# Attention and ELU feed-forward on one core: row sums issued together with the first half of AV, q and k copied from PSUM in one pass, loads and steps of the start reordered, dummy matmuls moved

## The chip, the core and the metric

The kernel runs on one core of a Trainium2 chip. The metric is the device time of one launch in microseconds (us); lower is better. A core has a tensor engine (PE, matrix products into the PSUM memory), a vector engine (DVE), a scalar engine (ACT), GpSimd (POOL, here it only makes masks and issues loads) and SyncE (SP, it issues the output stores). All five run at the same time, each its own list of instructions in order; semaphores join them. Times from the profile count from the start of the execution's span, which is some 1.7 us shorter than the time that is measured from outside.

## The reference

Attention over 8 batches of 8 heads, 576 queries, 16 "beacon" keys in front of 576 causal ones, head size 64; then a feed-forward layer with ELU on the 4608 x 512 result.

```python
k_all = concatenate([beacon_k, k]); v_all = concatenate([beacon_v, v])
scores = where(causal, -1e9, q @ k_all.T / 8)          # B,H = 8,8; S = 576; D = 64
a = exp(scores - max); a /= a.sum(-1) + 1e-9
x = (a @ v_all) laid out as [4608, 512]
h = x @ w_in                                           # 512 -> 2048
g = where(h > 0, h, exp(min(h, 0)) - 1)
out = g @ w_out                                        # 2048 -> 512
```

## The kernel before

The program is a list of small *steps*. Each step puts instructions on one engine, and the order of the list is the order of every engine's own program. `b` is a batch, `p` a pair of heads, `g` a part, `t` a tile of 512 tokens, `i` a piece of it.

- `T.b.p` (PE) transposes q and k of a pair into PSUM; `ck` (ACT) copies k out of PSUM, `cq` (DVE) copies q; `cb` (DVE) puts the beacon keys in front.
- `S.b.p.g` (PE) scores, `x` (ACT) exp, `m` (DVE) causal mask.
- `L.b.g` (PE) row sums of the exps, by a product with ones; `n` (ACT) turns them into 1/sum as exp(-Ln(sum)), so it holds the Ln; `W.b.g.half` (PE) product with v for one half of the head size (AV); `M` (DVE) multiplies AV by 1/sum into x. `R` (PE) does sums and AV for the last 64 queries, which do not fit one bank.
- `F.t.i` (PE) x @ w_in; `e` (ACT) exp; `r`, `g` (DVE) ELU; `G.t.tb.qd` (PE) g @ w_out; `o` (DVE), `s` (SP) copy and store.
- `lk`, `lv`: loads of q and k, of v. `warm.n`: n matmuls with zeros that only keep PE running.

The parts that the change and the argument touch (cuts marked `...`):

```python
psum = tc.tile_pool(name="psum", bufs=2, space=PSUM)   # tags: "S" 2 pairs of banks, "hps" 2 banks, "ops" 2 banks
...
new_stage(0); load_qk(0, ...) x4; new_stage(1); load_v(0, ...)
load_qk(1, 0, H // 2); load_wi(0, 1024); load_wi(1024, 2048); load_qk(1, H // 2, H)
load_wo(0); load_wo(1); load_wo(2); load_wo(3)
load_v(1, list(range(NKC)))
...
def T(b, p):
    if b == 0 and p < 3:
        tps[b, p] = bank("hps", BF16, "tq"), bank("hps", BF16, "tk")
    else:
        t = psum.tile([P, 2, 1024], BF16, tag="S", name="tp")    # one pair of banks: q and k
        tps[b, p] = t[:, 0, :], t[:, 1, :]
    ...
def ck(b, p):
    nc.scalar.copy(out=kTof[b, p][:, NB:SK]..., in_=tps[b, p][1][:, 0:S]...)
def cq(b, p):
    nc.vector.tensor_copy(out=qTof[b, p]..., in_=tps[b, p][0][:, 0:S]...)
def S_(b, p, g):
    ...
    if b == 0:
        nc.tensor.matmul(out=s[:, 0, :], lhsT=zero[:, 0:P], rhs=zero, ...)   # a dummy
    ...
def L(b, g):
    ...
    t = psum.tile([P, 2, 512], FP32, tag="S", name="lt")
    quad(b, g, 0, Q1, t[:, 0, :], None, True)
    lt[b, g], ut[b, g, 0] = t[:, 0, :], t[:, 1, :]     # sums in one bank, AV half 0 in the other
def W(b, g, *i):
    ...
    if half:
        t = psum.tile([P, 2, 512], FP32, tag="S", name="ut")
        ut[b, g, 1], ut[b, "R"] = t[:, 0, :], t[:, 1, :]   # AV half 1 in one bank, R in the other
    quad(b, g, 0, Q1, ut[b, g, half], half, True)
...
run(""" warm.12 bt bk cb.0.0 cb.0.1 T.0.0 ... (the start: some 420 steps by hand, batches 0 to 2) ... """)

def LW(b, g):
    run(f"L.{b}.{g} n.{b}.{g} W.{b}.{g}.0 M.{b}.{g}.0")
def WR(b, g):
    run(f"W.{b}.{g}.1 M.{b}.{g}.1")
    if g == 1:
        run(f"R.{b} n.{b}.R M.{b}.R")

SLOTS = [0, 1, 2, 4, 5, 6, 8, 9, 10, 11, 12, 13]
for b in range(3, NT // TT + 2):                       # the loop: one turn for one tile of tokens
    for i in range(NFC):                               # 16: F.b.i e r g, G of tile b-1, and at the slots:
        # SC(b,1,0) SC(b,1,2) T_(b,3)+LW(b,0) SC(b,2,0) SC(b,2,2) T_(b+1,0)+WR(b,0)
        # SC(b,3,0) SC(b,3,2) T_(b+1,1)+LW(b,1) SC(b+1,0,0) SC(b+1,0,2) T_(b+1,2)+WR(b,1)
```

Both PSUM pairs of `L` and `W` are one tile for the program. A step of one engine on a tile waits for the earlier steps of other engines on it, although they are at the other bank.

The softmax here doesn't subtract the row's maximum and nothing guards it: scores larger than these inputs give would overflow.

## Time and profile before

403.2 us, median of 3 runs (402.68 to 404.11).

| | before |
|---|---|
| span of the profiled run | 400.2 us |
| PE, DVE, ACT busy | 91%, 68%, 57% |
| the loop begins (first F of turn 3) | 113.1 us |
| a turn of the loop (turns 3 to 6) | 43.49 us |
| first F at all | 30.4 us |

PE does nearly all the time's work, so the question is where PE does not work. The page of the profile: busy us and instructions of each engine; then PE in 40 slices of the span (tenths; 9 is 90% or more) and the clock of PE that was granted.

```profile
PE 365.4 (91%) x4416; PEld 183.8 (46%) x4416; DVE 270.8 (68%) x640; ACT 227.6 (57%) x351; POOL 67.8 (17%) x100
...
PE   6889859989899998999899989999899999999995
...
PEclk9899969999999999999999999999999999999999
```

There is a hole near the sixth slice (50 to 60 us), with the clock low, and single 8s among the 9s of the loop. The waits of PE before: who waited for whom, us in total, times, longest.

```profile
PE lt L304 <- ACT rl L337: 8.9, 12, 0.9
PE ut L304 <- DVE xT L374: 7.0, 5, 1.5
PE tp L229 <- DMA qst<-in_q_dram: 3.1, 1, 3.1
PE tp L229 <- DMA kst<-in_k_dram: 2.1, 1, 2.1
PE sc L259 <- DVE qT L250: 1.9, 2, 1.1
...
PE sc L267 <- ACT kT_94 L243: 1.4, 2, 1.0
```

The first line is W.0 waiting for Ln, the second is R waiting for M, and both recur in the loop. The next two are T.2.0 waiting for q and k of batch 2; the last two are scores that wait for the copies `cq` and `ck`. The timeline of PE in turn 3 of before (start us, us of the group, ..., idle time ahead of it and its releaser) shows the two waits of the loop:

```profile
120.11 0.76 PE L304 MATMUL lt<-et,ones 128*32 128x512 f16 x20
121.59 0.76 PE L304 MATMUL lt<-et,v_1838 128*32 128x512 f16 x20 [0.72 <-ACT rl L337]
...
149.76 0.76 PE L304 MATMUL ut<-et,v_1838 128*32 128x512 f16 x20
152.01 0.48 PE L304 MATMUL ut<-et,ones 128*32 128x64 f16 x40 [1.50 <-DVE xT L374]
```

And stretches of before: us, then busy us of PE, PE weight loads, DVE, ACT, POOL (instructions), granted clock, DMA share (time of the packets over that of the 16 engines; it can pass 1), GB/s. The stretches are: first F to T.2.0, the wait at T.2.0, from there to the loop, and one turn.

```profile
30.40:49.10 18.70, 17.84 (x254) 12.07 (x252) 14.75 (x42) 15.69 (x24) 9.48 (x13) 1.00 1.50 191
49.10:55.60 6.50, 1.37 (x25) 1.06 (x26) 0.96 (x2) 0.86 (x1) 3.07 (x4) 0.70 1.32 204
55.60:113.10 57.50, 54.01 (x895) 30.13 (x894) 43.87 (x109) 39.88 (x63) 7.68 (x11) 0.97 0.61 75
156.60:200.10 43.50, 40.56 (x530) 19.95 (x529) 31.38 (x75) 27.23 (x42) 6.27 (x10) 1.00 0.49 67
```

### The profile page before, as it was taken

To read this page: it belongs to the slowest core of one execution; us is meant where nothing else is said; L and a number is where in the kernel's file an instruction comes from. 1 tells how busy PE (TensorE), PEld (TensorE's weight loads), DVE (VectorE), ACT (ScalarE), POOL (GpSimd) and SP (SyncE) were. 2 spreads that over 40 slices of the span, in tenths; PEclk is the share of its full clock that TensorE was granted. 3 is DMA by queue.
4 is the path that set the end of the run, shared out by engine and by line. 5 is a ranking of instruction groups with operands and counts; after the bars stand their busy time and mean duration, and the time that the engine had idled before them with its cause. 6 is when DMAs were issued, how large, how long until landed. Compare 5 with 4: busy or idle time off the path is not lost.

```text
span 400.2 us, 10284 instructions
## 1 busy us (share of the span) xinstructions
PE 365.4 (91%) x4416; PEld 183.8 (46%) x4416; DVE 270.8 (68%) x640; ACT 227.6 (57%) x351; POOL 67.8 (17%) x100
## 2 busy tenths in 40 slices
PE   6889859989899998999899989999899999999995
PEld 3347535544454444444444444444444444444442
DVE  2447826778786876776677776777677667767741
ACT  2889736678566664667466656667366533333300
POOL 8784520410041004100330004000000000000000
PEclk9899969999999999999999999999999999999999
DMA  8999997491098007830297009000001000010112
GB/s 121 172 187 198 184 200 51 56 148 60 29 62 146 28 29 53 118 87 7 40 88 134 28 29 89 28 26 28 25 5 54 20 34 27 29 52 26 55 52 79
DMA packets 61102, 28.84 MB, mean 72 GB/s; under 512 B 41088, under 2 KB 55424, under 8 KB 61056
## 3 DMA queue, kind: packets, MB, share of 16 engines
q0 software_dynamic: 54720, 18.49, 41.6%
q1 hardware_dynamic: 5760, 9.57, 6.5%
q8 instruction: 34, 0.56, 0.6%
q10 hardware_dynamic: 576, 0.13, 0.2%
q14 instruction: 12, 0.10, 0.1%
HBM read 37.22 MB, written 9.44 MB: 117 GB/s over the span
## 4 chain that ended last, share of the span: by engine, by line
PE 76%; DMA 8%; POOL 5%; ACT 4%; DVE 4%; issue 2%; POOLq 0%
PE hps L425 30%; PE ops L456 29%; PE sc L267 6%; PE lt L304 5%; DMA kst<-in_k_dram 4%; DMA w_out_80<-in_moe_w_out_dram 4%; PE ut L304 3%; PE tp L229 3%; ACT rl L337 2%; ACT et L277 1%; DVE qT L250 1%; POOL w_in_79 L138 1%; POOL v_124 L126 1%; DVE xT L374 1%; POOL qst L113 1%
## 5 line engine op out<-in xcount | busy, mean ns | idle before, releaser
L425 PE MATMUL hps<-xT,w_in_79 128*128 128x512 f16 (+1 forms) x640 | 148.8, 361 | 0.3
L456 PE MATMUL ops<-w_out_80,gt 128*128 128x512 f16 x576 | 145.1, 379 | 0.0
L435 ACT ACTIVATE e<-hps 128x512 f32<-128x512 f32 x144 | 86.3, 600 | 86.4 <-PE hps L425 86.0
L277 ACT ACTIVATE et<-sc 128x832 f16<-128x832 f32 x128 | 104.4, 863 | 19.4 <-PE sc L267 19.1
L447 DVE TENSOR_TENSOR gt<-hps,r 128x512 f16<-128x512 f32 x144 | 99.6, 691 | 6.2 <-PE sc L267 0.5
L456 PEld LDWEIGHTS <-gt 128*128 128x128 f16 x576 | 55.9, 98 | 66.5 <-issue 0.5
L440 DVE TENSOR_SCALAR r<-e 128x512 f16<-128x512 f32 x144 | 61.4, 427 | 36.7 <-ACT e L435 35.4
L425 PEld LDWEIGHTS <-w_in_79 128*128 128x128 f16 x640 | 56.8, 98 | 56.3 <-issue 5.1
L293 DVE TENSOR_TENSOR et<-et,triu 128x256 f16<-128x256 f16 (+3 forms) x164 | 40.7, 270 | 30.2 <-ACT et L277 30.1
L250 DVE COPY qT<-tp 128x576 bf16<-128x576 bf16 x29 | 21.9, 757 | 15.1 <-ACT kT_94 L243 8.3
L463 DVE COPY osb<-ops 128x512 f32<-128x512 f32 x36 | 24.5, 682 | 10.2 <-PE ops L456 10.2
L374 DVE TENSOR_TENSOR xT<-lt,rl 128x448 f16<-128x448 f32 (+6 forms) x28 | 10.6, 418 | 9.9 <-PE lt L304 9.5
L304 PEld LDWEIGHTS <-ones 128*32 128x32 f16 (+1 forms) x624 | 10.8, 96 | 12.0 <-issue 8.7
L229 PE MATMUL tp<-identb,qst 96*64 96x96 bf16 x348 | 13.1, 212 | 3.2 <-DMA qst<-in_q_dram 3.1
L229 PEld LDWEIGHTS <-qst 96*64 96x64 bf16 x384 | 10.3, 111 | 12.5 <-issue 8.6
L229 PE MATMUL tp<-identb,kst 96*64 96x96 bf16 x348 | 12.5, 209 | 2.1 <-DMA kst<-in_k_dram 2.1
L340 ACT ACTIVATE rl<-rl 128x512 f32<-128x512 f32 (+2 forms) x23 | 12.4, 537 | 0.7
L113 POOL DMA_DIRECT2D qst<-in_q_dram x12 | 8.7, 726 | 21.0 <-PE tp L229 16.6
L304 PE MATMUL lt<-et,ones 128*32 128x512 f16 (+7 forms) x320 | 11.8, 279 | 0.2 <-DVE qT L250 0.2
L229 PEld LDWEIGHTS <-kst 96*64 96x64 bf16 x384 | 10.7, 112 | 2.5 <-DMA kst<-in_k_dram 2.3
L337 ACT ACTIVATE rl<-lt 128x512 f32<-128x512 f32 (+1 forms) x15 | 9.0, 603 | 3.4 <-PE lt L304 2.5
L374 DVE TENSOR_TENSOR xT<-ut,rl 128x448 f16<-128x448 f32 (+6 forms) x28 | 10.4, 414 | 0.6 <-ACT rl L337 0.6
(95 smaller groups left out, 231.1 us busy)
## 6 DMA issues: line engine op xcount, KB each, us to landing
out_dram<-osb SPq DMA_DIRECT2D x36, 256.0 KB, 2.0
qst<-in_q_dram POOLq DMA_DIRECT2D x6, 576.0 KB, 6.2
kst<-in_k_dram POOLq DMA_DIRECT2D x6, 576.0 KB, 8.5
w_in_79<-in_moe_w_in_dram POOLq DMA_DIRECT2D x16, 128.0 KB, 5.1
w_out_80<-in_moe_w_out_dram POOLq DMA_DIRECT2D x4, 512.0 KB, 12.3
qst<-in_q_dram POOLq DMA_DIRECT2D x4, 144.0 KB, 4.5
kst<-in_k_dram POOLq DMA_DIRECT2D x4, 144.0 KB, 5.0
qst<-in_q_dram POOLq DMA_DIRECT2D x2, 288.0 KB, 6.0
```

The costliest lines, as they stand in the source:

```text
L229: nc.tensor.transpose(out=dst[D * h:D * (h + 1), PR * r:PR * (r + 1)], in_=src[:, 2 * p + h, r, :], identity=identb[0:PR, 0:PR],)
L250: nc.vector.tensor_copy(out=qTof[b, p].rearrange("c (p r) -> c p r", r=R), in_=tps[b, p][0][:, 0:S].rearrange("c (r p) -> c p r", r=R))
L277: nc.scalar.activation(out=ets[b, p][:, :, GW * g:GW * (g + 1)], in_=sc[b, p, g][:, :, 0:GW], func=AFT.Exp, bias=0.0, scale=SCALE)
L293: nc.vector.tensor_tensor(out=o, in0=o, in1=triu[0:kc[j], :, t0:t0 + e - a], op=ALU.mult)
L304: nc.tensor.matmul(out=t[32 * i:32 * (i + 1), a - qa:e - qa], lhsT=ones[0:kc[j], :] if half is None else v16[0:kc[j], j, h, 32 * half:32 * ...
L374: nc.vector.tensor_tensor(out=x_tile(k)[:, cc, tok - TT * k:to - TT * k], in0=u[:, o:o + to - tok], in1=r[:, o:o + to - tok], op=ALU.mult)
L425: nc.tensor.matmul(out=h[:, n_, :], lhsT=w_in16[:, cc, P * fc:P * (fc + 1)], rhs=xt[k][:, cc, a - TT * k:e - TT * k], start=(cc == 0), sto ...
L435: nc.scalar.activation(out=eb[t, i], in_=flat(hp[t, i]), func=AFT.Exp, bias=0.0, scale=1.0)
L440: nc.vector.tensor_scalar(out=rb[t, i], in0=eb[t, i], scalar1=1.0, scalar2=1.0, op0=ALU.min, op1=ALU.subtract)
L447: nc.vector.tensor_tensor(out=flat(gt), in0=flat(hp[t, i]), in1=rb[t, i], op=ALU.max)
L456: nc.tensor.matmul(out=ob[t, tb_], lhsT=gts[t, fc][:, P * tb_:P * (tb_ + 1)], rhs=w_out16[:, fc, :], start=(fc == 0), stop=(fc == NFC - 1))
L463: nc.vector.tensor_copy(out=osb, in_=ob[t, tb_])
```

## The change

Its intent: take the two waits out of the loop by order alone (W.0 before Ln; R before M), take one of two copies per pair away, bring q and k of batch 2 sooner, and spend PE's idle moments of the start on dummies that were placed for it, not in front of every score.

```diff
-    kTs = [konst.tile([P, P * NKC], BF16, name=f"kT{i}") for i in range(NKT)]
+    qks = [konst.tile([P, 2, P * NKC], BF16, name=f"qk{i}") for i in range(NQK)]
...
     load_qk(1, H // 2, H)
-    load_wo(0)
-    load_wo(1)
-    load_wo(2)
-    load_wo(3)
-    load_v(1, list(range(NKC)))
...
+    w0 = bank("ops", name="w0")
     @step
-    def warm(n):
-        w = bank("ops", name="w0")
+    def warm(n, rows=P):
         for _ in range(n):
-            nc.tensor.matmul(out=w, lhsT=zero[:, 0:P], rhs=zero, ...)
+            nc.tensor.matmul(out=w0, lhsT=zero[0:rows, 0:P], rhs=zero[0:rows, :], ...)
...
     def ck(b, p):
-        nc.scalar.copy(out=kTof[b, p][:, NB:SK]..., in_=tps[b, p][1][:, 0:S]...)
+        t = qkT[b, p]
+        if b == 0 and p < 3:
+            nc.scalar.copy(out=t[:, 1, NB:SK]..., in_=tps[b, p][1][:, 0:S]...)
+        else:                                              # q and k at once
+            nc.scalar.copy(out=t[:, :, NB:SK]..., in_=tps[b, p][:, :, 0:S]...)
...
     def S_(b, p, g):
-        if b == 0:
-            nc.tensor.matmul(out=s[:, 0, :], lhsT=zero[:, 0:P], rhs=zero, ...)
...
     run("""
-    warm.12 bt bk cb.0.0 cb.0.1 T.0.0 cb.0.3 cb.0.2 ck.0.0 cq.0.0 S.0.0.0 T.0.1 cq.0.1 x.0.0.0
+    warm.12 bt bk cb.0.0 cb.0.1 cb.0.3 cb.0.2 warm.3 T.0.0 ck.0.0 cq.0.0 warm.4.64 S.0.0.0 S.0.0.1
...
+    warm.2.64 T.0.3 wo.0 wo.1 lv.1 lk.2 wo.2 wo.3 m.0.0.3 x.0.1.2 S.0.1.3 ck.0.2 m.0.1.0 m.0.1.2
... (the rest of the start in a new order; 24 dummies of 64 rows in it; q's copies gone but three)
     def LW(b, g):
-        run(f"L.{b}.{g} n.{b}.{g} W.{b}.{g}.0 M.{b}.{g}.0")
+        run(f"L.{b}.{g} W.{b}.{g}.0 n.{b}.{g} M.{b}.{g}.0")
     def WR(b, g):
-        run(f"W.{b}.{g}.1 M.{b}.{g}.1")
-        if g == 1:
-            run(f"R.{b} n.{b}.R M.{b}.R")
+        run(f"W.{b}.{g}.1" + g * f" R.{b}" + f" M.{b}.{g}.1" + g * f" n.{b}.R M.{b}.R")
-    SLOTS = [0, 1, 2, 4, 5, 6, 8, 9, 10, 11, 12, 13]
+    SLOTS = [0, 1, 2, 4, 5, 6, 7, 8, 9, 11, 12, 13]
```

The texts below speak of 26 small dummies; the list of after has 24.

More of the change, by code (lines that the diff above doesn't have):

```diff
@@ L152 @@
     nc.vector.memset(ones, 1.0)
-    NKT = 4
-    kTs = [konst.tile([P, P * NKC], BF16, name=f"kT{i}") for i in range(NKT)]
-    for kt in kTs:
-        nc.vector.memset(kt[:, SK:P * NKC], 0.0)
+    NQK = 4
+    qks = [konst.tile([P, 2, P * NKC], BF16, name=f"qk{i}") for i in range(NQK)]
+    for t in qks:
+        nc.vector.memset(t[:, 1, SK:P * NKC], 0.0)
     identb = konst.tile([P, P], BF16)
@@ L194, in bank @@
         return psum.tile([P, 512 if dt == FP32 else 1024], dt, tag=tag, name=name)
+    w0 = bank("ops", name="w0")
     @step
-    def warm(n):
-        w = bank("ops", name="w0")
+    def warm(n, rows=P):
         for _ in range(n):
-            nc.tensor.matmul(out=w, lhsT=zero[:, 0:P], rhs=zero, start=True, stop=True, skip_group_check=True)
+            nc.tensor.matmul(
+                out=w0, lhsT=zero[0:rows, 0:P], rhs=zero[0:rows, :], start=True, stop=True, skip_group_check=True)
     tb = []
@@ L214, in bk @@
         nc.vector.tensor_copy(out=bkT, in_=tb[0][:, 0:NP * P])
-    tps, kTof, qTof, sc, ets = {}, {}, {}, {}, {}
-    kseq = [0]
+    tps, qkT, sc, ets = {}, {}, {}, {}
+    seq = [0]
     @step
@@ L222, in T @@
             tps[b, p] = bank("hps", BF16, "tq"), bank("hps", BF16, "tk")
+            dsts = tps[b, p]
         else:
-            t = psum.tile([P, 2, 1024], BF16, tag="S", name="tp")
-            tps[b, p] = t[:, 0, :], t[:, 1, :]
-        for dst, src in zip(tps[b, p], st[b]):
+            tps[b, p] = psum.tile([P, 2, 1024], BF16, tag="S", name="tp")
+            dsts = tps[b, p][:, 0, :], tps[b, p][:, 1, :]
+        for dst, src in zip(dsts, st[b]):
             for r in range(R):
@@ L236, in cb @@
     def cb(b, p):
-        kTof[b, p] = kTs[kseq[0] % NKT]
-        kseq[0] += 1
-        nc.vector.tensor_copy(out=kTof[b, p][:, 0:NB], in_=bkT[:, p, NB * b:NB * (b + 1)])
+        qkT[b, p] = qks[seq[0] % NQK]
+        seq[0] += 1
+        nc.vector.tensor_copy(out=qkT[b, p][:, 1, 0:NB], in_=bkT[:, p, NB * b:NB * (b + 1)])
     @step
     def ck(b, p):
-        nc.scalar.copy(
-            out=kTof[b, p][:, NB:SK].rearrange("c (p r) -> c p r", r=R),
-            in_=tps[b, p][1][:, 0:S].rearrange("c (r p) -> c p r", r=R))
+        t = qkT[b, p]
+        if b == 0 and p < 3:
+            nc.scalar.copy(
+                out=t[:, 1, NB:SK].rearrange("c (p r) -> c p r", r=R),
+                in_=tps[b, p][1][:, 0:S].rearrange("c (r p) -> c p r", r=R))
+        else:
+            nc.scalar.copy(
+                out=t[:, :, NB:SK].rearrange("c i (p r) -> c i p r", r=R),
+                in_=tps[b, p][:, :, 0:S].rearrange("c i (r p) -> c i p r", r=R))
     @step
     def cq(b, p):
-        qTof[b, p] = attn.tile([P, S], BF16, tag="qT", bufs=4, name="qT")
         nc.vector.tensor_copy(
-            out=qTof[b, p].rearrange("c (p r) -> c p r", r=R),
+            out=qkT[b, p][:, 0, NB:SK].rearrange("c (p r) -> c p r", r=R),
             in_=tps[b, p][0][:, 0:S].rearrange("c (r p) -> c p r", r=R))
@@ L257, in S_ @@
         s = sc[b, p, g] = psum.tile([P, 2, 512], FP32, tag="S", name="sc")
-        if b == 0:
-            nc.tensor.matmul(out=s[:, 0, :], lhsT=zero[:, 0:P], rhs=zero, start=True, stop=True, skip_group_check=True)
-        qT, kT = qTof[b, p], kTof[b, p]
+        t = qkT[b, p]
         c0, c1 = GW * g, GW * (g + 1)
@@ L268, in S_ @@
                     out=s[:, h, a - c0:e - c0],
-                    lhsT=kT[D * h:D * (h + 1), P * j:P * (j + 1)],
-                    rhs=qT[D * h:D * (h + 1), qa + a - col:qa + e - col],
+                    lhsT=t[D * h:D * (h + 1), 1, P * j:P * (j + 1)],
+                    rhs=t[D * h:D * (h + 1), 0, NB + qa + a - col:NB + qa + e - col],
                     start=True, stop=True, skip_group_check=True,
@@ L471, in lk, with wo @@
     @step
+    def wo(i):
+        load_wo(i)
+    @step
     def lk(b):
@@ L487 @@
     run("""
-    warm.12 bt bk cb.0.0 cb.0.1 T.0.0 cb.0.3 cb.0.2 ck.0.0 cq.0.0 S.0.0.0 T.0.1 cq.0.1 x.0.0.0
-    S.0.0.1 ck.0.1 x.0.0.1 m.0.0.0 S.0.0.2 x.0.0.2 S.0.1.0 S.0.1.1 x.0.1.0 T.0.2 x.0.1.1 T.0.3
-    ck.0.2 S.0.0.3 m.0.0.2 ck.0.3 x.0.0.3 m.0.1.0 cq.0.3 S.0.1.2 S.0.1.3 cb.1.0 x.0.1.2 x.0.1.3
-    S.0.3.0 cq.0.2 x.0.3.0 m.0.0.3 S.0.2.0 x.0.2.0 m.0.1.2 cb.1.1 m.0.1.3 S.0.3.1 m.0.3.0 S.0.3.2
-    x.0.3.1 S.0.3.3 x.0.3.2 m.0.2.0 x.0.3.3 S.0.2.1 x.0.2.1 L.0.A W.0.A.0 cb.1.2 m.0.3.2 T.1.0 n.0.A
@@ L493 @@
-    ck.1.0 S.0.2.2 m.0.3.3 cq.1.0 W.0.A.1 S.0.2.3 x.0.2.2 x.0.2.3 S.1.0.0 M.0.A.0 M.0.A.1 m.0.2.2
-    cb.1.3 W.0.B.0.0 T.1.1 m.0.2.3 x.1.0.0 cq.1.1 W.0.B.0.1 ck.1.1 S.1.0.1 S.1.1.0 x.1.0.1 x.1.1.0
-    F.0.0 m.1.0.0 e.0.0 m.1.0.1 m.1.1.0 F.0.1 r.0.0 S.1.0.2 e.0.1 L.0.B x.1.0.2 g.0.0 n.0.B F.0.2
-    r.0.1 g.0.1 F.0.3 m.1.0.2 M.0.B.0.0 e.0.2 S.1.1.1 S.1.0.3 M.0.B.0.1 e.0.3 cb.2.0 W.0.B.1.0
-    x.1.1.1 r.0.2 g.0.2 r.0.3 W.0.B.1.1 g.0.3 S.1.1.2 M.0.B.1.1 x.1.0.3 F.0.5 F.0.4 x.1.1.2 e.0.5
-    M.0.B.1.0 T.1.2 lk.2 m.1.1.2 r.0.5 e.0.4 g.0.5 T.1.3 F.0.6 m.1.1.1 cq.1.2 ck.1.2 r.0.4 S.1.1.3
@@ L499 @@
-    ck.1.3 G.0.0.0 cq.1.3 x.1.1.3 S.1.3.0 cb.2.1 g.0.4 e.0.6 m.1.0.3 S.1.3.1 x.1.3.0 r.0.6 F.0.7
-    G.0.1.0 x.1.3.1 e.0.7 S.1.2.0 S.1.2.1 x.1.2.0 g.0.6 x.1.2.1 F.1.2 m.1.3.0 m.1.1.3 m.1.3.1 e.1.2
-    r.0.7 g.0.7 m.1.2.0 G.0.0.1 m.1.2.1 r.1.2 S.1.2.2 T.2.0 x.1.2.2 F.1.0 g.1.2 S.1.3.2 ck.2.0 e.1.0
-    cq.2.0 S.1.2.3 x.1.3.2 m.1.2.2 x.1.2.3 cb.2.2 r.1.0 g.1.0 F.1.4 G.0.0.2 e.1.4 m.1.3.2 m.1.2.3
-    r.1.4 S.2.0.0 g.1.4 T.2.1 F.1.1 x.2.0.0 ck.2.1 m.2.0.0 cq.2.1 G.0.1.1 S.2.0.1 L.1.0 e.1.1 r.1.1
@@ L504 @@
-    x.2.0.1 g.1.1 n.1.0 m.2.0.1 W.1.0.0 T.2.2 F.1.5 ck.2.2 F.1.7 cq.2.2 M.1.0.0 e.1.5 r.1.5 S.1.3.3
-    x.1.3.3 g.1.5 S.2.0.2 G.0.0.3 cb.2.3 S.2.0.3 m.1.3.3 e.1.7 F.1.3 x.2.0.2 x.2.0.3 W.1.0.1 o.0.0
-    lk.3 L.1.1 cb.3.0 W.1.1.0 r.1.7 m.2.0.2 g.1.7 M.1.0.1 e.1.3 n.1.1 W.1.1.1 lv.2 m.2.0.3 R.1 r.1.3
-    n.1.R g.1.3 M.1.1.0 F.1.6 G.0.1.2 e.1.6 M.1.1.1 S.2.2.0 M.1.R r.1.6 x.2.2.0 S.2.1.0 g.1.6
-    m.2.2.0 F.2.2 F.2.0 x.2.1.0 e.2.2 m.2.1.0 S.2.1.1 S.2.1.2 e.2.0 r.2.2 x.2.1.1 g.2.2 r.2.0 g.2.0
-    m.2.1.1 x.2.1.2 G.1.0.0 G.1.0.1 T.2.3 T.3.0 ck.2.3 F.2.1 m.2.1.2 cq.2.3 S.2.3.0 cq.3.0 ck.3.0
@@ L510 @@
-    e.2.1 S.2.2.1 G.0.1.3 r.2.1 F.2.4 x.2.3.0 g.2.1 x.2.2.1 e.2.4 S.2.1.3 m.2.3.0 o.0.1 S.2.3.1
-    m.2.2.1 cb.3.2 F.2.3 r.2.4 x.2.3.1 G.1.0.2 e.2.3 x.2.1.3 g.2.4 F.2.7 m.2.3.1 r.2.3 g.2.3 S.2.2.2
-    m.2.1.3 e.2.7 S.2.3.2 r.2.7 s.0.0 F.2.5 g.2.7 x.2.3.2 m.2.3.2 x.2.2.2 G.1.1.0 F.2.6 m.2.2.2
-    e.2.5 r.2.5 S.3.0.0 S.2.3.3 G.1.0.3 e.2.6 x.3.0.0 g.2.5 r.2.6 g.2.6 x.2.3.3 lv.3 F.2.9 S.3.0.1
-    e.2.9 x.3.0.1 m.3.0.0 o.1.0 m.2.3.3 S.2.2.3 x.2.2.3 cb.3.1 F.2.11 r.2.9 g.2.9 G.1.1.1 S.3.0.2
-    e.2.11 s.1.0 S.3.0.3 m.3.0.1 F.2.8 m.2.2.3 G.1.1.2 x.3.0.2 r.2.11 g.2.11 m.3.0.2 x.3.0.3 F.2.13
@@ L516 @@
-    m.3.0.3 G.1.1.3 e.2.8 e.2.13 r.2.8 g.2.8 F.2.10 r.2.13 g.2.13 T.3.1 e.2.10 ck.3.1 s.0.1 L.2.1
-    W.2.1.0 n.2.1 o.1.1 cq.3.1 r.2.10 L.2.0 n.2.0 g.2.10 W.2.0.0 F.2.12 M.2.1.0 e.2.12 F.2.14 e.2.14
-    W.2.0.1 M.2.0.0 s.1.1 W.2.1.1 r.2.12 R.2 g.2.12 M.2.0.1 T.3.2 r.2.14 g.2.14 ck.3.2 M.2.1.1 n.2.R
-    F.2.15 cq.3.2 e.2.15 M.2.R r.2.15 g.2.15
+    warm.12 bt bk cb.0.0 cb.0.1 cb.0.3 cb.0.2 warm.3 T.0.0 ck.0.0 cq.0.0 warm.4.64 S.0.0.0 S.0.0.1
+    T.0.1 x.0.0.0 cq.0.1 m.0.0.0 x.0.0.1 S.0.0.2 warm.1.64 S.0.0.3 ck.0.1 x.0.0.2 cb.1.0 warm.1.64
@@ new lines @@
+    T.0.2 S.0.1.0 x.0.0.3 x.0.1.0 warm.1.64 S.0.1.1 m.0.0.2 cq.0.2 x.0.1.1 warm.2.64 S.0.1.2
+    warm.2.64 T.0.3 wo.0 wo.1 lv.1 lk.2 wo.2 wo.3 m.0.0.3 x.0.1.2 S.0.1.3 ck.0.2 m.0.1.0 m.0.1.2
+    ck.0.3 warm.5.64 S.0.3.0 x.0.1.3 warm.2.64 S.0.2.0 cb.1.1 x.0.3.0 m.0.1.3 x.0.2.0 m.0.3.0
+    warm.2.64 S.0.3.1 warm.2.64 S.0.2.1 x.0.3.1 m.0.2.0 x.0.2.1 warm.2.64 S.0.3.2 x.0.3.2 L.0.A
+    S.0.3.3 n.0.A x.0.3.3 cb.1.3 m.0.3.2 W.0.A.1 T.1.0 M.0.A.1 m.0.3.3 W.0.A.0 S.0.2.2 W.0.B.0.1
+    ck.1.0 M.0.A.0 x.0.2.2 S.0.2.3 cb.1.2 T.1.1 x.0.2.3 m.0.2.2 S.1.0.0 ck.1.1 m.0.2.3 F.0.0 e.0.0
@@ new lines @@
+    r.0.0 F.0.3 x.1.0.0 g.0.0 m.1.0.0 W.0.B.1.1 e.0.3 S.1.0.1 S.1.1.0 x.1.0.1 F.0.2 r.0.3 x.1.1.0
+    e.0.2 g.0.3 L.0.B m.1.0.1 m.1.1.0 n.0.B S.1.1.1 F.0.1 r.0.2 g.0.2 F.0.5 M.0.B.0.1 M.0.B.1.1
+    x.1.1.1 S.1.1.2 S.1.0.2 W.0.B.0.0 m.1.1.1 e.0.1 r.0.1 x.1.1.2 e.0.5 W.0.B.1.0 lv.2 g.0.1 x.1.0.2
+    M.0.B.0.0 S.1.0.3 F.0.7 x.1.0.3 e.0.7 cb.2.0 T.1.2 r.0.5 m.1.1.2 m.1.0.2 ck.1.2 T.1.3 g.0.5
+    m.1.0.3 r.0.7 F.0.4 ck.1.3 g.0.7 e.0.4 M.0.B.1.0 S.1.1.3 F.0.6 cb.2.1 x.1.1.3 G.0.0.0 lk.3 r.0.4
+    g.0.4 e.0.6 m.1.1.3 r.0.6 S.1.3.0 S.1.3.1 x.1.3.1 g.0.6 F.1.1 m.1.3.1 e.1.1 x.1.3.0 G.0.1.0
@@ new lines @@
+    F.1.0 r.1.1 g.1.1 S.1.3.2 e.1.0 m.1.3.0 r.1.0 x.1.3.2 S.1.2.0 x.1.2.0 F.1.2 G.0.0.1 g.1.0 e.1.2
+    S.1.3.3 S.1.2.1 m.1.3.2 F.1.5 m.1.2.0 x.1.3.3 cb.2.2 x.1.2.1 r.1.2 S.1.2.2 e.1.5 g.1.2 F.1.3
+    m.1.3.3 G.0.1.1 x.1.2.2 m.1.2.1 r.1.5 e.1.3 g.1.5 m.1.2.2 S.1.2.3 r.1.3 T.2.0 x.1.2.3 ck.2.0
+    g.1.3 F.1.6 F.1.7 S.2.0.0 S.2.0.1 e.1.6 cb.3.0 x.2.0.0 x.2.0.1 G.0.0.2 S.2.0.2 m.1.2.3 x.2.0.2
+    G.0.1.2 T.2.1 r.1.6 g.1.6 e.1.7 m.2.0.0 T.2.2 m.2.0.1 ck.2.1 m.2.0.2 G.0.0.3 ck.2.2 L.1.0 r.1.7
+    W.1.0.0 g.1.7 S.2.0.3 o.0.0 n.1.0 cb.2.3 F.1.4 M.1.0.0 x.2.0.3 e.1.4 m.2.0.3 G.0.1.3 r.1.4
@@ new lines @@
+    W.1.0.1 o.0.1 L.1.1 M.1.0.1 g.1.4 W.1.1.0 n.1.1 W.1.1.1 M.1.1.0 R.1 S.2.1.0 M.1.1.1 x.2.1.0
+    G.1.1.0 n.1.R m.2.1.0 M.1.R F.2.1 F.2.0 e.2.1 S.2.1.1 S.2.1.2 e.2.0 r.2.1 g.2.1 G.1.1.1 r.2.0
+    F.2.2 x.2.1.1 S.2.2.0 x.2.1.2 S.2.2.1 g.2.0 m.2.1.1 e.2.2 F.2.3 x.2.2.0 m.2.1.2 x.2.2.1 r.2.2
+    G.1.0.0 e.2.3 g.2.2 m.2.2.0 m.2.2.1 r.2.3 F.2.4 S.2.2.2 g.2.3 e.2.4 S.2.1.3 cb.3.2 x.2.2.2 r.2.4
+    g.2.4 G.1.1.2 F.2.5 m.2.2.2 T.3.0 x.2.1.3 m.2.1.3 e.2.5 T.2.3 ck.3.0 ck.2.3 F.2.6 r.2.5 G.1.1.3
+    g.2.5 e.2.6 S.2.2.3 S.2.3.0 F.2.8 o.1.1 cb.3.1 x.2.2.3 G.1.0.1 r.2.6 x.2.3.0 S.2.3.1 m.2.2.3
@@ new lines @@
+    L.2.0 e.2.8 x.2.3.1 W.2.0.0 g.2.6 W.2.0.1 m.2.3.0 s.0.0 r.2.8 g.2.8 s.0.1 m.2.3.1 F.2.7 n.2.0
+    M.2.0.1 e.2.7 M.2.0.0 F.2.9 S.3.0.0 e.2.9 S.2.3.2 lv.3 G.1.0.2 r.2.7 g.2.7 x.3.0.0 x.2.3.2
+    F.2.11 S.3.0.1 e.2.11 x.3.0.1 r.2.9 m.3.0.0 g.2.9 m.2.3.2 r.2.11 g.2.11 s.1.1 S.2.3.3 m.3.0.1
+    F.2.10 x.2.3.3 G.1.0.3 e.2.10 S.3.0.2 m.2.3.3 o.1.0 x.3.0.2 S.3.0.3 F.2.12 r.2.10 m.3.0.2 g.2.10
+    L.2.1 e.2.12 W.2.1.0 x.3.0.3 s.1.0 r.2.12 F.2.14 g.2.12 m.3.0.3 n.2.1 M.2.1.0 F.2.13 e.2.14
+    T.3.1 W.2.1.1 e.2.13 r.2.14 R.2 ck.3.1 T.3.2 g.2.14 r.2.13 F.2.15 g.2.13 M.2.1.1 n.2.R M.2.R
@@ L520 @@
+    e.2.15 r.2.15 ck.3.2 g.2.15
     """)
@@ L523, in T_ @@
         if b < B:
-            run(f"cb.{b}.{p} T.{b}.{p} ck.{b}.{p} cq.{b}.{p}")
+            run(f"cb.{b}.{p} T.{b}.{p} ck.{b}.{p}")
     def SC(b, p, g0):
```

## The prediction

> **What bounds it now.** The tensor engine (PE) is busy 365.4 of 400.2 us (91%, busy table) and holds 76% of the chain that ended last. DVE (68%) and ACT (57%) have room. Time is lost in two places.
>
> 1. *The loop* (from about 113 us, table of stretches). A turn takes 43.50 us at full clock, PE busy 40.56. The waits view names the 2.94 us: the first AV half (W.0) waits 0.72 us, twice a turn, for Ln to read the row sums ("PE lt <- ACT rl": 8.9 us, 12 times); the remainder block R waits 1.50 us for the multiply M that reads the other half of its PSUM pair ("PE ut <- DVE xT": 7.0 us, 5 times). These are different banks of one tile, so program order makes the wait.
> 2. *The start* (0 to 113 us). I estimate 85 us of PE work, from the loop's durations: three batches at 12.9 us, 43 us of F and G. Lost: PE waits 3.1 + 2.1 us for q and k of batch 2 (49 to 55 us), which queue behind all of w_out and v (k lands at 54.9); the granted clock is then 0.66 in 50 to 60 us; 16 zero matmuls before scores take 6.8 us; two row-sum pairs wait 0.76 and 0.87 us. The Trainium skill ("TensorE: Matmul & The Clock Gate", part 1) says that an idle window of about 3.4 us halves the clock; this trace agrees: F pairs take 1.82 us after the gap, 0.98 us later.
>
> **What changes.**
> - L, W.0, Ln, M; and W.1, R, M, Ln: both loop waits go. Turns 3 to 6 gain 2.94 us, turn 7 gains 2.4 (its R waits 0.98): 14.2 us, all on the chain.
> - q and k in one ACT pass: 576 elements more on a 640 ns copy. The Trainium skill ("ScalarE: Activation LUTs", cost of ACTIVATE) gives 0.833 ns per element, so about 1.12 us; the traced 640 ns agrees with its 186 ns + 480. DVE loses copies of 757 ns that followed the ACT copy. ACT +2 us, DVE -3 us per turn: off the chain.
> - Loads: q and k of batch 2 go ahead of half of w_out (1.05 MB, 5.5 us at the traced 190 GB/s), so k lands near 50, and 6 us more matmuls precede T.2.0: that wait vanishes.
> - Dummies: 16 full ones out, 26 half-row ones into gaps, 3 full ones before the first transpose (0.3 to 0.6 us late). They should keep the clock near 1.0 (now 0.80 at 14 to 20 us). The first F should start near 27 us instead of 30.4; w_in's first half lands near 26.
> - ACT is nearly the limit at 9 to 50 us (8 to 9 of 10 busy) and gets 2.4 us more there.
>
> Start in sum: load wait 5, low clock 1.5, row-sum waits 1.7, earlier F 2 to 3, less 2 for ACT and dummies: about 9 us (4 to 12); the loop begins near 104.
>
> **Prediction: 380 us** (403.2 - 14.2 - 9), 8 in 10 between 375.5 and 386. Faster by over 2%: 0.97; within 2%: 0.02; slower: 0.01.
>
> **Signs.** Right: turns of 40.5 to 40.8 us; no PE wait on rl or xT in the loop; 128x1152 copies near 1.12 us; no PE wait on loads after 45 us and clock 1.0 at 50 to 60. Wrong if: the start is bound by ACT (loop starts after 109); dummies delay scores; the copy across two banks takes over 1.2 us; w_out's second half stops G; a turn stays over 41.5 because ACT delays F's release.

## The result, and the profile after

After took 372.64 us (median of 4, 372.22 to 372.84), before 403.65 us in the same rounds (median of 4, 402.68 to 404.44). The ratio is 0.9231 (95% interval 0.9207 to 0.9256). Ratios are the mean time of one kernel's fast runs over that of the other's of the same rounds, so they are not quite the ratio of the medians. The gain is 31.0 us; 23.2 were predicted, and 372.64 lies below the range. The direction and the main mechanisms were right, their size was not.

| | before | after | gain |
|---|---|---|---|
| span of the profiled run | 400.2 | 371.1 | 29.1 |
| start: until the loop begins | 113.1 | 100.2 | 12.9 |
| turns 3 to 7 | 213.9 | 197.7 | 16.2 |
| turns 8 on, and the end | 73.3 | 73.3 | 0 |

(The times are those of the first F matmul of turns 3 and 8 in the two traces: 113.07 and 326.97, 100.22 and 297.88.) The page of after, the same lines as of before:

```profile
PE 361.5 (97%) x4427; PEld 182.1 (49%) x4427; DVE 251.9 (68%) x611; ACT 238.5 (64%) x351; POOL 68.4 (18%) x100
...
PE   8989989999999999999999999999999999999995
...
PEclk9999999999999999999999999999999999999999
```

The waits of PE, after:

```profile
PE tp L229 <- DMA kst<-in_k_dram: 1.3, 1, 1.3
PE w_151 L198 <- DVE zero L150: 1.3, 1, 1.3
PE sc L271 <- ACT et L281: 1.1, 3, 0.7
...
PE ut L308 <- DVE xT L378: 0.3, 1, 0.3
```

The two lines of the loop are gone, and so are the waits for copies. Turn 3 of after in the timeline:

```profile
107.27 0.76 PE L308 MATMUL lt<-et,ones 128*32 128x512 f16 x20
107.87 0.74 PE L308 MATMUL lt<-et,v_1917 128*32 128x512 f16 x20
...
135.13 0.76 PE L308 MATMUL ut<-et,v_1917 128*32 128x512 f16 x20
135.73 0.49 PE L308 MATMUL ut<-et,ones 128*32 128x64 f16 x40
```

Compare the *starts*, not the idle times. From L to W.0 there were 1.48 us before (120.11 to 121.59) and there are 0.60 now: 0.88 less, while the profile had listed 0.72 of idle time. From W.1 to R there were 2.25 us and are 0.60 now: 1.65 less for 1.50 listed. The other 0.15 us of each wait lie inside the row: a group of 20 matmuls that takes 0.60 us when the next one follows is shown as 0.76 us. (The profile models the ends of PE's rows, so the starts are the safer reading.) The stretches of after (first F to T.2.0, T.2.0, from there to the loop):

```profile
26.10:50.03 23.93, 23.93 (x333) 16.17 (x332) 19.03 (x53) 22.62 (x33) 15.19 (x20) 1.00 1.42 186
50.03:52.10 2.07, 0.80 (x28) 0.62 (x24) 1.94 (x7) 0.86 (x1) 0.12 (x1) 1.00 1.24 206
52.10:100.20 48.10, 47.11 (x845) 25.34 (x841) 33.98 (x86) 37.89 (x56) 9.54 (x13) 1.00 0.86 107
```

From the first F to T.2.0, PE is busy 23.93 of 23.93 us although ACT is busy 22.62 of them. Over the whole start, PE's idle time fell from 16.6 us (113.1 less 96.5 busy, the sum over the stretches) to 5.5 us (100.2 less 94.7): 11.1 of the start's 12.9 us.

### The profile page after: what moved, and what is told of

It is laid out like the page before. It is cut to its first block, busy times and chain, and to the rows that moved or that the text cites. A ratio compares the mean times of both kernels' runs of the same rounds, so it can differ in the third digit from the quotient of the medians.

```text
span 371.1 us, 10275 instructions
## 1 busy us (share of the span) xinstructions
PE 361.5 (97%) x4427; PEld 182.1 (49%) x4427; DVE 251.9 (68%) x611; ACT 238.5 (64%) x351; POOL 68.4 (18%) x100
## 4 chain that ended last, share of the span: by engine, by line
PE 88%; DMA 5%; POOL 4%; issue 1%; DVE 1%; ACT 1%; POOLq 0%
PE hps L429 34%; PE ops L460 33%; PE sc L271 7%; PE lt L308 5%; DMA kst<-in_k_dram 5%; PE tp L229 4%; PE ut L308 4%; POOL v_124 L126 1%; DMA w_in_79<-in_moe_w_in_dram 1%; POOL qst L113 1%; POOL kst L113 1%; DVE xT L378 1%; PE ub L308 0%; POOL w_in_79 L138 0%; ACT rl L344 0%
## 5 line engine op out<-in xcount | busy, mean ns | idle before, releaser
L281 ACT ACTIVATE et<-sc 128x832 f16<-128x832 f32 x128 | 104.2, 872 | 16.3 <-PE sc L271 16.2
L444 DVE TENSOR_SCALAR r<-e 128x512 f16<-128x512 f32 x144 | 63.7, 442 | 31.5 <-ACT e L439 29.7
L297 DVE TENSOR_TENSOR et<-et,triu 128x256 f16<-128x256 f16 (+2 forms) x164 | 40.7, 270 | 25.8 <-ACT et L281 25.5
L198 PE MATMUL w_151<-zero 64*128 64x512 bf16 (+1 forms) x39 | 13.0, 454 | 1.3 <-DVE zero L150 1.3
L229 PE MATMUL tp<-identb,qst 96*64 96x96 bf16 x348 | 12.9, 209 | 0.4 <-ACT et L281 0.4
```

The costliest lines, as they stand in the source:

```text
L229: nc.tensor.transpose(out=dst[D * h:D * (h + 1), PR * r:PR * (r + 1)], in_=src[:, 2 * p + h, r, :], identity=identb[0:PR, 0:PR],)
L281: nc.scalar.activation(out=ets[b, p][:, :, GW * g:GW * (g + 1)], in_=sc[b, p, g][:, :, 0:GW], func=AFT.Exp, bias=0.0, scale=SCALE)
L297: nc.vector.tensor_tensor(out=o, in0=o, in1=triu[0:kc[j], :, t0:t0 + e - a], op=ALU.mult)
L444: nc.vector.tensor_scalar(out=rb[t, i], in0=eb[t, i], scalar1=1.0, scalar2=1.0, op0=ALU.min, op1=ALU.subtract)
```

## The experiments

The change has five parts that can be told apart: (1) the order in the loop, with its slots; (2) the single copy of q and k; (3) the loads; (4) the order of steps in the start; (5) the dummies. Each run undoes one in after, or puts one or two into before. "Loop begins" is the first F of turn 3 in the run's trace. The runs came in four blocks, each on one chip with the kernel before beside them: from loop_order_alone to gap_dummies_out, from loop_order_and_slots to start_order_alone, from loads_alone to loads_q_k_first, and the last two.

| run | median us | ratio to before (95%) | loop begins | turns 3, 4, 5, 6 |
|---|---|---|---|---|
| before | 403.65 | 1 | 113.1 | 43.5, 43.5, 43.5, 43.5 |
| after | 372.64 | 0.9231 (0.9207 to 0.9256) | 100.2 | 40.1, 40.3, 40.3, 40.1 |
| loop_order_alone | 388.33 | 0.9614 (0.9559 to 0.9669) | 113.9 | 40.5, 40.5, 40.5, 40.3 |
| loop_order_undone | 388.21 | 0.9620 (0.9569 to 0.9671) | 99.2 | 43.5, 43.5, 43.5, 43.5 |
| copies_split | 377.58 | 0.9349 (0.9305 to 0.9393) | 103.6 | 41.4, 40.3, 40.3, 40.1 |
| gap_dummies_out | 374.65 | 0.9277 (0.9226 to 0.9328) | 101.5 | 40.1, 40.3, 40.3, 40.1 |
| loop_order_and_slots | 386.33 | 0.9592 (0.9546 to 0.9637) | 113.6 | 40.3, 40.3, 40.3, 40.1 |
| loads_undone | 378.98 | 0.9388 (0.9347 to 0.9428) | 106.7 | 40.1, 40.3, 40.3, 40.1 |
| single_pass_alone | 404.95 | 1.0039 (0.9999 to 1.008) | 114.7 | 44.2, 43.5, 43.5, 43.5 |
| start_order_alone | 397.26 | 0.9846 (0.9808 to 0.9883) | 106.7 | 44.8, 43.5, 43.5, 43.5 |
| loads_alone | 397.88 | 0.9881 (0.9838 to 0.9924) | 110.2 | 43.5, 43.5, 43.5, 43.5 |
| loads_and_single_pass | 397.52 | 0.9879 (0.9845 to 0.9913) | 107.6 | 44.2, 43.5, 43.5, 43.5 |
| zeros_for_gap_dummies | 372.82 | 0.9264 (0.9237 to 0.9291) | 100.2 | 40.1, 40.3, 40.3, 40.1 |
| loads_q_k_first | 372.84 | 0.9267 (0.9237 to 0.9296) | 100.0 | 40.3, 40.3, 40.3, 40.1 |
| after_same_chip | 373.09 | 0.9255 (0.9235 to 0.9275) | 100.4 | 40.1, 40.3, 40.3, 40.1 |
| dummies_out_same_chip | 374.47 | 0.9302 (0.9274 to 0.9330) | 101.0 | 40.1, 40.3, 40.3, 40.1 |

The median of before differs by up to 1.6 us from block to block (402.52 to 404.12), so differences of 1 or 2 us are only read within one block. All outputs were correct.

### 1. The order in the loop, alone in before

```diff
-        run(f"L.{b}.{g} n.{b}.{g} W.{b}.{g}.0 M.{b}.{g}.0")
+        run(f"L.{b}.{g} W.{b}.{g}.0 n.{b}.{g} M.{b}.{g}.0")
   (and WR as in the change; SLOTS as before)
```

> The kernel before with only the new order in the loop (L, W.0, Ln, M and W.1, R, M, Ln). Theory A, a removed wait of PE also takes away the emptying and refilling of the array, 0.15 us each: turns of 40.1 us and about 16.2 us less than before (387 us). Rival B, a removed wait is worth just the idle time that the waits view shows (2.94 us a turn): turns of 40.55 us and 14.2 us less (389 us). If the new slots or the single ACT copy are needed for it, turns stay above 41.

388.33 us against 404.12, turns of 40.5 us for 43.5. By the turns alone this looks like rival B (40.55). The starts say otherwise: L to W.0 and W.1 to R start 0.60 us apart as in after (201.90 to 202.50, 230.00 to 230.60), which is theory A, and a part is given back elsewhere; that B's number came out is chance. PE's timeline of this run:

```profile
222.03 0.74 PE L304 MATMUL lt<-et,v 128*32 128x512 f16 x20
...
224.54 0.76 PE L267 MATMUL sc<-qT,kT 64*128 64x416 bf16 x6
```

The last line is a group of scores one F and one G behind L and W; the same six matmuls take 0.53 us at the other slots. So the next run moved the slots.

```diff
-    SLOTS = [0, 1, 2, 4, 5, 6, 8, 9, 10, 11, 12, 13]
+    SLOTS = [0, 1, 2, 4, 5, 6, 7, 8, 9, 11, 12, 13]
```

> The kernel before with the new order in the loop and the new slots (a step's scores at 7, 8, 11 instead of 8, 9, 10). The order alone gave turns of 40.49 us, not the 40.1 of theory A: there scores come one step after T, L and W, and their second pair waits for a buffer (a score group of 0.76 us instead of 0.53 at 224.54). If that is all, turns are now 40.07 us and the time is about 2 us under the order alone. If the single copy is needed for the rest, turns stay near 40.5.

Turns of 40.27, 40.25, 40.26 and 40.06 us, the same as after's later turns. So order and slots give the whole gain of the loop without the single copy. The slots are worth 0.23 us a turn by the traces, half of what was expected; the 2.0 us between the two medians come from two chips and are not read as more. The rest of 0.2 us, which two of after's four turns have too (40.26 against 40.06), was not looked into.

### 2. The order in the loop, undone in after

```diff
-        run(f"L.{b}.{g} W.{b}.{g}.0 n.{b}.{g} M.{b}.{g}.0")
+        run(f"L.{b}.{g} n.{b}.{g} W.{b}.{g}.0 M.{b}.{g}.0")
   (and WR as before)
```

> The kernel after with the old order in the loop. If the parts simply add: turns of 43.5 us, about 389 us. Theory: the 1.12 us copy of q and k stands on ACT just in front of Ln, where the copy of k took 0.64 us, so with the old order Ln ends about 0.45 us later and W.0 waits near 1.2 us instead of 0.72, twice a turn: turns of about 44.4 us, about 392.5 us. The order and the single copy would then need one another.

388.21 us and turns of 43.5 us: the parts add, and the theory that they need one another fell. Half of it was seen: Ln does come later behind the copy of 1.12 us, and W.0 waits 1.02 us instead of 0.72.

```profile
PE lt L308 <- ACT rl L341: 9.9, 10, 1.0
PE ut L308 <- DVE xT L378: 4.8, 6, 1.0
```

But R now waits at most 1.0 us for M instead of 1.5, because no copy of q stands on DVE in front of M. Two times 0.30 more and 0.5 less cancel.

### 3. Copies split again

```diff
   def ck(b, p): nc.scalar.copy(k only)
+  cq.b.p (DVE copies q) behind each ck.b.p
```

> The kernel after with q copied by DVE and k by ACT again, the order kept. Theory A: in the start the pair of copies in series (0.64 + 0.76 us) kept the scores waiting, and the single pass took most of the 4.6 us of PE waits on copies away: 3 to 5 us slower than after in the start (the loop begins at 103 to 105 us), turns still 40.1. Rival B: the new order of the start hides the copies whatever they take: less than 1 us slower.

377.58 us against 372.64 (other block; 373.09 in a third): some 4.5 to 5 us slower. The loop begins at 103.6 us, 3.4 later, and turn 3 takes 1.4 us more: the size that theory A gave for the start. Its reason was wrong. The waits of PE are these:

```profile
PE hps L424 <- DVE gt L446: 4.2, 5, 1.6
PE sc L266 <- DVE qk L251: 1.8, 3, 0.9
```

Only 1.8 us are scores that wait for copies. 4.2 us are F, waiting for `g` on DVE, which frees its bank. DVE's timeline shows how, and PE's below it:

```profile
38.73 0.76 DVE L251 COPY qk<-tp 128x576 bf16<-128x576 bf16 x1 [1.34 <-ACT qk L245]
39.40 0.68 DVE L446 TENSOR_TENSOR gt<-hps,r 128x512 f16<-128x512 f32 x1
...
40.13 1.03 PE L424 MATMUL hps<-xT,w_in 128*128 128x256 f16 x8 [1.61 <-DVE gt L446]
```

DVE's copy of q waits 1.34 us for ACT's copy of k (the program runs the two copies of one pair of banks one after the other), and everything behind it in DVE's list waits as well. The single pass is worth its time as the removal of a step that blocked a queue, more than as a shorter copy. The 5 us hold for this list, which was arranged without q's copies; a list arranged anew for split copies was not tried. (The split copies here write after's one tile for q and k; before has two tiles, and there too DVE's copies waited for ACT's.)

### 4. The single pass, alone in before

```diff
   def ck(b, p): for b > 0 or p == 3, q and k in one nc.scalar.copy, as in the change; those cq steps taken out
   (loads, order, dummies and loop as before)
```

> The kernel before with only the single ACT pass for q and k. Taking it out of after cost 4.9 us. Theory (wall of loads): before, PE stands at T.2.0 until k lands at 54.9 us whatever it did earlier, so what the single pass gains ahead of that is lost there; only the copies after 55 us count: 0.5 to 1.5 us faster than before, the wait at T.2.0 longer by what was gained. In the loop Ln comes later (W.0 waits about 1.0 us) and R waits less (about 1.0 us): turns of 43.5 us. Rival (parts add): about 4.9 us faster.

404.95 us against 403.52, ratio 1.0039 (0.9999 to 1.008): worth nothing, perhaps a little less than that; the 0.5 to 1.5 us of the theory were not seen. The first F came at 28.6 us instead of 30.4, so 1.9 us were gained there. Then:

```profile
PE tp L232 <- DMA qst<-in_q_dram: 6.2, 1, 6.2
PE tp L232 <- DMA kst<-in_k_dram: 2.2, 1, 2.2
```

The wait at T.2.0 grew from 3.1 + 2.1 us to 6.2 + 2.2 us. T.2.0's k arrived at 56.3 us in this run (54.9 in the trace of before; why it came later was not looked into). Until it arrives, whatever was gained is waited away. The trace of loop_order_alone, whose start is that of before, shows the same without any change of the start: its first F came at 29.3 us, 1.2 us earlier, it waited 4.5 + 2.2 us at T.2.0, and its loop began no earlier (113.9 us). That is the theory of a wall of loads, and the rival that parts add fell for the start.

### 5. The loads, undone in after and alone in before

```diff
   (undone in after)
     load_qk(1, H // 2, H)
+    for i in range(4): load_wo(i)
+    load_v(1, list(range(NKC)))
-    ... T.0.3 wo.0 wo.1 lv.1 lk.2 wo.2 wo.3 ...
+    ... T.0.3 lk.2 ...
```

> The kernel after with the old order of loads (all of w_out and v of batch 1 ahead of q and k of batch 2). Theory: T.2.0 is reached at 50.0 us and k lands near 55 us as before, so PE waits 4 to 5 us there and its clock drops: loop begins at 104 to 106 us, 4 to 6 us slower than after. Rival: the loads land earlier anyway because the transposes free their buffers sooner, and less than 1.5 us comes back.

378.98 us, the loop begins at 106.7 us instead of 100.2. PE waits at T.2.0 as before:

```profile
PE tp L232 <- DMA kst<-in_k_dram: 2.6, 1, 2.6
PE tp L232 <- DMA qst<-in_q_dram: 1.1, 1, 1.1
```

k landed at 55.1 us. The two times come from two chips; by the traces the loop begins 6.5 us later than in after, a little more than the 4 to 6 us that were expected. Only 2.5 us of it are the longer wait (3.7 against 1.3). Another 2.6 us are the clock behind the wait: it was granted at 0.50 from 54.5 to 61.2 us, and from the F behind T.2.0 to T.2.1 the same matmuls took 7.14 us (55.72 to 62.86) for 4.53 in after (52.12 to 56.65). 0.8 us had been lost ahead of T.2.0.

```diff
   (alone in before: load_wo and load_v(1) out of the top, and behind T.0.3:)
+    T.0.3 wo.0 wo.1 lv.1 lk.2 wo.2 wo.3
```

> The kernel before with only the new order of loads. Theory (wall of loads): k of batch 2 lands near 52 us instead of 54.9; T.2.0 is reached at 49 us as before, so PE waits about 2 to 3 us instead of 5.2 and loses less clock: 3 to 4.5 us faster than before. If both the wall and the rest of the start matter equally, the loop begins near 109.5 us.

397.88 us against 402.52: 4.6 us faster. k landed at 51.7 us, and the wait at T.2.0 fell from 5.2 to 0.7 + 2.4 us. As the theory had it, a little over its 3 to 4.5 us.

```diff
   (loads as above, and the single pass of experiment 4)
```

> The kernel before with the new loads and the single pass. The single pass alone was worth nothing (404.95 us). Theory: with the wall moved to about 52 us, the 1.9 us that it gains before the first F still run into the wait for k, so only a part comes out: 0 to 1.5 us faster than loads_alone. Rival (the 4.9 us that it was worth in after come back as soon as the loads are earlier): 4 us or more faster than loads_alone.

397.52 us against 397.88 for the loads alone, on the same chip: no difference, as the wall asks for. In this pair of profiles the loop began 2.6 us earlier, but q and k of batch 2 also happened to land earlier there (k at 49.9 us), and turn 3 gave 0.75 back; the four timed runs do not show it.

### 6. The order of the start, alone in before

```diff
-    (the start's list of before)
+    (the start's list of after, with cq steps, without dummies; one tile for q and k as in after;
+     loads, zeros in S, LW, WR and SLOTS as before)
```

> The kernel before with only the new order of steps in the start (old copies, old loads, zero matmuls in front of scores, old loop). Theory: the new order puts about 6 us of matmuls ahead of T.2.0, so the wait for k there (5.2 us) nearly vanishes although k still lands near 55 us: the loop begins at 106 to 109 us instead of 113.1, 4 to 7 us faster than before. Rival: without the single pass and the loads the order stalls elsewhere (F on g, scores on copies): less than 2 us faster.

397.26 us against 403.52, the loop begins at 106.7: 6.3 us faster. With the new list PE came to T.2.0 at 55.7 us, and did not wait for the loads at all:

```profile
55.73 0.45 PE L232 MATMUL tp<-identb,qst 96*64 96x96 bf16 x12
```

Two things brought it there that late. The list has more matmuls ahead of T.2.0 (from the first F to it after took 23.93 us and before 18.70), and PE lost time on the way: after gets there with the same list at 50.0 us. F waited for `g` on DVE, as in experiment 3, 2.6 us of it ahead of T.2.0:

```profile
PE hps L429 <- DVE gt L451: 4.6, 6, 1.7
```

So the order moves the wall's position in the program, the loads move the wall, and only then does the single pass pay. The loop begins at 106.7 us with the order alone, at 106.7 with order, single pass and dummies but old loads (loads_undone), at 103.6 with order, loads and dummies but split copies, and at 100.2 with all.

### 7. The dummies

```diff
-    warm.4.64 ... warm.1.64 ... (all 24)
```

> The kernel after without the 26 half-row dummies in the gaps (the 15 full ones at the very start stay). If they hold the clock: granted clock falls to 0.6 to 0.9 between 10 and 25 us, the first F starts 1 to 2 us later, 1 to 2.5 us slower. If ACT sets the pace there (it is 93% busy from 7.4 to 26.1 us after the change): the clock falls, but the first F stays within 0.5 us of 26.1 and the time within 0.7 us of after.

374.65 us, but after had been timed on another chip, and the intervals of the two ratios overlap. So both were run again side by side:

> The kernel after itself, as a control on the chip of the next run. If chips differ only in their kernel before (start with load waits), it takes 372 to 373.5 us again.

> The kernel after without the 26 gap dummies, on the same chip as the control. If the dummies hold the clock and this counts: 1.3 to 2.5 us slower than the control (the traces' loops began at 101.5 and 100.2 us). If the 2 us were the chip's: within 0.5 us of the control.

373.09 us (372.82 to 373.34) and 374.47 us (373.67 to 377.17): the ranges do not touch, so taking the dummies out costs about 1.4 us. The stretches of the last run (columns as above; the third number from the end is the granted clock):

```profile
7.40:14.00 6.60, 4.60 (x105) 3.13 (x104) 4.34 (x15) 4.92 (x7) 6.60 (x10) 0.95 1.66 156
14.00:20.00 6.00, 4.13 (x54) 2.81 (x54) 2.32 (x13) 6.00 (x9) 3.63 (x7) 0.50 1.55 192
```

and of after:

```profile
7.40:14.00 6.60, 5.95 (x117) 3.90 (x117) 4.04 (x16) 5.36 (x8) 6.60 (x10) 1.00 1.68 155
14.00:20.00 6.00, 5.80 (x73) 2.87 (x68) 2.31 (x14) 6.00 (x9) 3.24 (x7) 1.00 1.46 186
```

Without them the clock is halved from 14 to 20 us, and yet the first F comes only 0.7 us later (26.94 us against 26.26 in the control): ACT is busy for all 6.00 of those 6.00 us in both, and PE, even at half clock, is not what the stretch waits for.

Nor do the traces show that the 1.4 us are the clock's. The run without dummies did not wait for k at T.2.0, and its next F came 0.4 us ahead of the control's (51.72 against 52.09 us); at T.3.1 it was 0.7 us ahead (95.50 against 96.19). It lost 1.3 us at one place, in the middle of R of batch 2, at full clock. The last matmuls of R there, first of this run and then of the control:

```profile
99.32 0.23 PE L308 MATMUL ut<-et,v 128*32 128x64 f16 x5 [1.47 <-issue]
...
98.53 0.41 PE L308 MATMUL ut<-et,v 128*32 128x64 f16 x29 [0.20 <-issue]
```

"issue" means that the profile shows nothing that PE waited for. The trace of gap_dummies_out has a gap of 1.27 us at the same matmul (99.83 us); after has 0.42 us in this R. Why this R stops longer in the kernel without dummies is open.

```diff
   (gap dummies out, and in S, as before:)
+        if b == 0:
+            nc.tensor.matmul(out=s[:, 0, :], lhsT=zero[:, 0:P], rhs=zero, ...)
```

> The kernel after with the 16 zero matmuls in front of batch 0's scores in place of the 26 half-row dummies. Without either it took 374.65 us, with the 26 dummies 372.64. Theory: any filler that keeps the clock up will do, but these stand in front of a score that waits for nothing but them: clock 0.8 to 1.0 at 10 to 25 us, first F within 0.7 us of 26.1, 372.6 to 374 us. If zeros delay the scores: over 374.5 us.

372.82 us (after took 372.64 and 373.09 on other chips), clock 1.00 throughout: the old zeros do as well as the planned dummies, as far as runs on different chips can tell. Their first F came at 26.93 us, a little later than expected and as late as without any filler, and the time did not suffer. So a later first F is not what costs the 1.4 us, and that a filler helps by holding the clock is argued, not shown.

### 8. An attempt to beat after

```diff
-    T.0.3 wo.0 wo.1 lv.1 lk.2 wo.2 wo.3
+    T.0.3 wo.0 wo.1 lk.2 wo.2 wo.3 lv.1
```

> An attempt to beat after: q and k of batch 2 go ahead of v of batch 1 too (w_out 0 and 1, q, k, w_out 2 and 3, then v). k landed at 51.7 us in after and PE waited 1.3 us for it. Theory: k lands near 48 us, no PE wait at T.2.0, w_out and v still in time (first used at 54.4 and 59.4 us): 0.5 to 1.5 us faster than after, about 371.5 us. If v then comes late, W of batch 1 waits and it is slower.

PE did not wait at T.2.0, and the time was 372.84 us (372.67 to 374.08), between after's 372.64 and 373.09 on two other chips. It is not shown to be better; the 0.5 to 1.5 us that were expected were not seen. The wait of 1.3 us in after's profile is not in every run either: it was 0.8 us in the control's trace and absent in that of loop_order_undone, whose start is the same.

## Why the prediction was wrong

The prediction named the right places (two waits of a turn, the loads of batch 2, the low clock) and the right direction, but gave 380 us with a low end of 375.5, and it was 372.64. The steps that failed are sizes in its sum: the gain of the loop was put 2.0 us too low (item 1), that of the start 3.9 us, 2 of them a deduction that did not come (items 2 and 3), and the base 1.9 us (item 4). Together these are the 7.8 us between 23.2 and 31.0.

1. *"both loop waits go. Turns 3 to 6 gain 2.94 us, turn 7 gains 2.4 ...: 14.2 us"*. The waits went, but the term was mis-sized: it measured 16.2 us (213.9 to 197.7). Each wait costs about 0.15 us more than the idle time that is listed for it. The Trainium skill ("TensorE: Matmul & The Clock Gate", section "Single matmul latency") gives a constant of about 166 ns for one matmul at full clock, and its section "Step-by-step: what each phase is for" says that back-to-back matmuls hide the time in which the array empties; the trace agrees with 0.16 us (1.48 less 0.60, less the 0.72 listed). Three waits a turn make some 0.45 us. The signs "turns of 40.5 to 40.8" failed for this reason (40.06 to 40.26), and loop_order_and_slots showed it without the other parts.
2. *"Start in sum: ... about 9 us"*. It measured 12.9 us. Term by term, from the two traces: the load wait gave 3.9 us, not 5 (5.2 to 1.3; "no PE wait on loads after 45 us" failed in this trace). The row-sum waits gave 1.4 us (1.6 to 0.3 us), as predicted within 0.3. The first F came 4.3 us earlier (26.1 for 30.4), not 2 to 3, and it did not wait for w_in; two other traces with the start of before have it at 29.3 and 30.0. Waits for copies behind the first F (0.5, 1.0 and 0.25 us at 42.6, 85.0 and 105.1 us of before) had been left out; they are gone. The low clock behind T.2.0 is gone as well. An estimate of it from the trace of before: the clock was 0.50 until 58.6 us and PE worked without a wait from 54.9 us on, so half of these 3.7 us, some 1.8 us, was lost (1.5 predicted). These terms add to 13.1 us.
3. *"less 2 for ACT and dummies"*. This deduction failed. ACT was busy 95% of the time from the first F to T.2.0 (22.62 of 23.93 us) and PE did not wait for it. The pass did add to ACT, but it took work and a blocking wait off DVE. A step that blocks DVE's list cost F 4.2 us in copies_split. The prediction counted the single pass as "off the chain", which is right for the loop (loop_order_and_slots, with split copies, has after's turns within 0.2 us) and wrong for the start, where taking it out cost 3.4 us (and 1.4 in turn 3); it pays only once order and loads have moved the wall, and the 5 us hold for a list arranged for it.
4. *The base.* The gains were read from a profiled run of 401.99 us and taken from a median of 403.2; the median in the timed rounds was 403.65. Before varies more (401.5 to 406.3 us in all blocks) than after (372.2 to 373.3). That is the last 1.9 us: the medians differ by 31.0 us, the two profiled spans by 29.1.
5. *Dummies.* With them the clock is 1.00, as predicted. Taking them out costs 1.4 us, but the traces put the loss at a gap near 99 us and not in the stretch with the low clock, and the old zeros took the same time. The first transpose started 0.17 us later (7.38 for 7.21), not 0.3 to 0.6. Copies of 128 x 1152 took 1.11 to 1.23 us, most of them 1.12; that sign held nearly throughout, and with it the estimate from the Trainium skill ("ScalarE: Activation LUTs", section "What ACT_TABLE_LOAD costs").

What stays open: the parts of the start are not independent, so no split of its 12.9 us into five numbers exists; the runs give what each part is worth alone and what is lost without it. The clock behind T.2.0 was measured in loads_undone (2.6 us) and only estimated in before. Why the kernel without dummies loses its time near 99 us is not known.

## What to carry to other kernels

Where two engines share a tile, give the engine that limits everything its next piece of work before the other engine's step, and read the worth of a removed wait from start to start, not from the listed idle time. In a pipeline's start, find the wall (here the landing of q and k of batch 2) before crediting gains ahead of it: what is gained in front of a wall is waited away there, and a part that measures nothing alone (the single pass, experiment 4) can cost 5 us to take out once the wall is moved (experiment 3). When a run is slower, find in its trace where it falls behind before naming the cause. A step that waits at the head of an in-order queue costs what stands behind it, so look at what it blocks and not only at its own length.

## What the Trainium skill lacked or had wrong

- "TensorE: Matmul & The Clock Gate" (the table of rules and "HAM oscillation"): the rule is no PE-idle gap over about 3 us. Without the gap dummies the clock fell to 0.50 before 14 us although no single wait of PE between 7 and 26 us in the trace of gap_dummies_out was longer than 0.75 us; PE was busy 4.60 of the 6.60 us from 7.4 to 14 us in the repeated run, and transposes ran for 2.10 us of it. The page's "second HAM failure mode" speaks of frequent short idles but gives no share; here 5.63 of 6.60 us (zeros_for_gap_dummies) and 5.95 of 6.60 us (after) held 1.00. These runs give no threshold either: from 14 to 20 us, 4.45 of 6.00 us busy went with 1.00 (zeros_for_gap_dummies) and 4.57 of 6.00 us with 0.80 (before). How far transposes count, of which the page's Part 4 speaks, was not separated.
- The same page gives the constant of about 166 ns, but neither it nor "Perfetto Trace Analysis" says that the idle time in front of a matmul understates a removed wait by it: 0.72 us listed, 0.88 us gained; 1.50 listed, 1.65 gained.
- The same page ("Terms") puts the cost of a low clock at the throttled time times (1 - K/N), and does not say that PE must limit the stretch. In dummies_out_same_chip the clock was 0.50 from 13.3 to 23.5 us, for which that gives an estimated 5.1 us; with ACT busy 10.17 of these 10.20 us, the first F came 0.7 us later than in the control, and the F behind T.2.0 0.4 us earlier.
